# One issue order for every engine, taken from an offline list schedule, in an attention plus gated-FFT kernel; trigonometry folded onto PE and ACT; a 76-row score contraction

## Chip, cores and metric

The kernel runs on one core of a Trainium2 chip. The metric is device microseconds of one execution. A core has engines that run on their own and meet at semaphores: PE (matmul), DVE (vector), ACT (activations), POOL (GpSimd), and SP, whose queue here issues the transfers that are not weight loads. Times are medians of several executions; profiles are of one execution. A run counts as slow when it is over 1.5% above the fastest run of the same kernel.

## The reference

Block-sparse causal attention, then a gated long convolution done through an FFT over the sequence. Cut to what matters:

```python
B, H, S, D = 4, 8, 768, 64          # q, k, v: float32 [B, H, S, D]
k_rep = k.reshape(B, H, 12, 64, D).mean(axis=3)          # one mean key per block of 64
gate  = q @ k_rep^T, causal by block
keep  = the 3 best blocks of each query, plus its own block, and causal inside
attn  = softmax(where(keep, q @ k^T / 8, -1e9)) @ v
x     = attn as [B, S, 512]
x1, x2, x3 = split(x @ w_proj)                           # w_proj [512, 1536]
conv  = irfft(rfft(x2, axis=1) * rfft(filter, axis=0))   # over S
out   = (x1 * conv * x3) @ w_out                         # w_out [512, 512], float32
```

## The kernel before

Heads are handled in 16 pairs, four to a batch. Each pair passes through *prep* (PE transposes of q and k, block sums, gate matmuls, top-3 selection, a mask written as 12 extra rows beside the 64 rows of q and k), then *attention* (scores, exp, values, normalization, transposition into xT and its even and odd halves xe, xo). Each batch then passes through *hyena*: x2p projection, forward DFT with the multiplications of the spectrum, x13p projection, inverse DFT, output projection. While one batch's attention runs, the hyena of the batch before it runs between its pieces, and preps run two pairs ahead. The interleaving is a weighted merge of Python generators, and the build's scheduler re-sorts the merged program on all engines but SP:

```python
    def merge(streams):
        while True:
            live = [s_ for s_ in streams if s_.alive]
            if not live:
                return
            min(live, key=lambda s_: s_.key()).step()      # least advanced stream first
    ...
            streams = [Stream(attn_gen(st), T_ATT),
                       Stream(later_preps(b), NP * (T_PREP + 0.1))]
            ...
                streams.append(Stream(hyena_gen(prev), T_HY))
            merge(streams)
    ...
        with tc.manual_schedule(engines={mybir.EngineType.SP}):
            schedule()
```

Inside prep, the block sums become a float16 pair (kmb) on DVE, and the gate matmuls need them:

```python
            nc.vector.tensor_copy(km[r, 0, cc], ks[r, :])
            nc.vector.tensor_tensor(km[r, 1, cc], ks[r, :], km[r, 0, cc], op=ALU.subtract)
    ...
                nc.tensor.matmul(gn[:, 32 * c:32 * c + 24], lhsT=qx[:, P * c:P * (c + 1)],
                                 rhs=km[:, w, 0:24], start=(n_ == 0), stop=(n_ == 3))
```

Inside hyena, the spectrum comes first and the x13 projection only after it:

```python
        for c in range(HC):
            xa = ms_tile("xa")
            dft_fwd(x2[0], x2[1], c, 0, xa)
            nc.vector.tensor_mul(t1, xa, HA[:, c, :])      # and t4; then xb, t3, t2
            nc.gpsimd.tensor_add(Y[:, 3 * c + 1, :], t3, t4)
            re_eng.tensor_sub(Y[:, 3 * c, :], t1, t2)
        [... cut ...]
            for dc in range(DC):
                yield from x13(dc)
                yield from conv(dc)
```

Cosines and sines are made at the start: an outer product on PE, three DVE operations that reduce the angle, one ACT sine. The scores contract over all 128 rows of two tiles whose rows 64 to 127 were filled beforehand on DVE, ACT and POOL:

```python
                nc.vector.tensor_scalar(ka, in0=pr[:, 0:HS], scalar1=1.0 / S, scalar2=MAGIC,
                                        op0=ALU.mult, op1=ALU.add)
                nc.vector.tensor_scalar(kb, in0=ka, scalar1=-MAGIC, scalar2=-float(S),
                                        op0=ALU.add, op1=ALU.mult)
                nc.vector.tensor_tensor(kb, kb, pr[:, 0:HS], op=ALU.add)
                nc.scalar.activation(F[:, t, HS * hf:HS * (hf + 1)], kb, AF.Sin, bias=0.0,
                                     scale=TWO_PI / S)
```

The softmax here doesn't subtract the row's maximum and nothing guards it: scores larger than these inputs give would overflow.

Of the kernel before, what the change touches and what calls it, by code (L numbers as in the profile page):

```python
# [15 lines left out]

@with_exitstack
def kernel(
# [10 lines left out]
    nc = tc.nc  # L29

    B, H, S, D = q.shape
    P = 128
    NQ = S // P
    NB = S // 64
    NP = H // 2
    Dm = H * D
# [8 lines left out]
    MANUAL = False  # L45
    TWO_PI = 2.0 * math.pi

# [3 lines left out]
    qkT = ctx.enter_context(tc.tile_pool(name="qkT", bufs=2))  # L51
# [12 lines left out]
    tail = {"on": False, "n": 0}  # L64

# [3 lines left out]
    def ms_tile(name, dtype=FP32):  # L69
        if tail["on"]:  # L70
            tail["n"] += 1
            if tail["n"] % 3 == 0:
                return sc_tile(name)[:, 0:512]
        return ps_ms.tile([P, 512 if dtype == FP32 else 1024], dtype, name=name, tag="ms")


    id32 = const.tile([P, P], FP32)
    make_identity(nc, id32)
    id16 = const.tile([P, P], FP16)
    nc.vector.tensor_copy(id16, id32)  # L80

    NS = 6
# [3 lines left out]


    eblk = const.tile([P, S], FP16)
    nc.vector.memset(eblk[64:P, :], 0.0)
    nc.vector.memset(eblk[64:76, :], EMASK)  # L90
    nc.gpsimd.affine_select(
        out=eblk[64:76, :], in_=eblk[64:76, :], compare_op=ALU.is_ge,
        fill=0.0, base=0, pattern=[[1, S]], channel_multiplier=-64)
    nc.gpsimd.affine_select(
        out=eblk[64:76, :], in_=eblk[64:76, :], compare_op=ALU.is_ge,
        fill=0.0, base=63, pattern=[[-1, S]], channel_multiplier=64)

    for t_ in kmb:
        nc.vector.memset(t_, 0.0)

    def fill_slot_pool(sl):
        nc.gpsimd.memset(Qt[sl][64:P, :, :], 0.0)
        nc.gpsimd.affine_select(
            out=Kt[sl][64:P, :, :],
            in_=eblk[64:P, :].rearrange("p (o s) -> p o s", o=1).to_broadcast([P - 64, 2, S]),
            compare_op=ALU.is_ge, fill=0.0, base=0, pattern=[[0, 2], [0, S]], channel_multiplier=0)

    def fill_slot(sl):
        nc.vector.memset(Qt[sl][64:P, :, :], 0.0)
        for t in range(2):  # L110
            (nc.vector.tensor_copy if t else nc.scalar.copy)(Kt[sl][64:P, t, :], eblk[64:P, :])

    fill_slot(0)


# [7 lines left out]
    nc.vector.memset(rowv, 1.0)  # L123
    nc.vector.memset(colv, COS)
    nc.vector.memset(cv3[:, :, 1, :], SIN)
    nc.vector.memset(cv4[:, :, 1, :], SIN)
    nc.vector.memset(colv[:, P:P + 1], COS)
    nc.gpsimd.iota(rowv[0:1, :], pattern=[[1, HS]], base=0, channel_multiplier=0,  # L128
                   allow_small_or_imprecise_dtypes=True)
    nc.gpsimd.iota(cv3[0:1], pattern=[[1, 2], [0, 2], [2, P]], base=0, channel_multiplier=0,  # L130
                   allow_small_or_imprecise_dtypes=True)
    nc.gpsimd.iota(cv4[0:1], pattern=[[1, 2], [0, 2], [2, 64]], base=256, channel_multiplier=0,
                   allow_small_or_imprecise_dtypes=True)
    nc.vector.memset(colv[0:1, P:P + 1], 384.0)
    crow = const.tile([P, 1], FP32)
    nc.gpsimd.memset(crow, 2.0 / S)
    nc.gpsimd.memset(crow[0:1, :], 1.0 / S)
# [3 lines left out]

    def trig_gen():
        for t in range(HC):
            for hf in range(2):
                pr = ms_tile("trigp")
                nc.tensor.matmul(pr[:, 0:HS], lhsT=rowv[:, P * t:P * (t + 1)],
                                 rhs=colv[:, HS * hf:HS * (hf + 1)], start=True, stop=True)
                ka = hy2.tile([P, HS], FP32, name="trig", tag="ce")
                kb = hy2.tile([P, HS], FP32, name="kb", tag="prod", bufs=4)
                nc.vector.tensor_scalar(ka, in0=pr[:, 0:HS], scalar1=1.0 / S, scalar2=MAGIC,  # L150
                                        op0=ALU.mult, op1=ALU.add)
                nc.vector.tensor_scalar(kb, in0=ka, scalar1=-MAGIC, scalar2=-float(S),
                                        op0=ALU.add, op1=ALU.mult)
                nc.vector.tensor_tensor(kb, kb, pr[:, 0:HS], op=ALU.add)
                nc.scalar.activation(F[:, t, HS * hf:HS * (hf + 1)], kb, AF.Sin, bias=0.0,
                                     scale=TWO_PI / S)
                yield 1.2

    def trig_back():
        for t in range(6):  # L160
            gq = ms_tile("gq", FP16)
            for u in range(HC):
                nc.tensor.transpose(gq[:, P * u:P * (u + 1)], F[:, u, P * t:P * (t + 1)], id16)
            nc.vector.tensor_copy(G[:, t, :], gq[:, 0:HS])
            yield 0.2


# [4 lines left out]
    HA0 = const.tile([P, Dm], FP16)  # L172

    def dft_fwd(xe, xo, c, kind, pt):

        if c < 2:
            src = xe if c == 0 else xo
            col = 256 * c + 128 * kind
            for t in range(HC):
                nc.tensor.matmul(pt, lhsT=F[:, t, col:col + P], rhs=src[:, t, :],  # L180
                                 start=(t == 0), stop=(t == HC - 1))
        else:
            for t in range(HC):
                for r, src in ((0, xe), (64, xo)):
                    col = 512 + 2 * r + 64 * kind
                    nc.tensor.matmul(pt[r:r + 64, :], lhsT=F[:, t, col:col + 64],
                                     rhs=src[:, t, :], start=(t == 0), stop=(t == HC - 1),
                                     skip_group_check=True)

    fts = []  # L190

    def load_filter():
        for t in range(HC):
            f0 = hy2.tile([P, Dm], FP32, name="f0", tag="t", bufs=6)
            f1 = hy2.tile([P, Dm], FP32, name="f1", tag="t", bufs=6)
            nc.sync.dma_start(f0, moe_filter_fft[P * t:P * (t + 1), :])
            nc.sync.dma_start(f1, moe_filter_fft[HS + P * t:HS + P * (t + 1), :])
            fts.append((f0, f1))

    wsrc = moe_w_proj.rearrange("(c p) n -> p c n", p=P)  # L200

    def load_w(part):
        nc.gpsimd.dma_start(wp[:, :, Dm * part:Dm * (part + 1)], wsrc[:, :, Dm * part:Dm * (part + 1)])

    def filter_gen():
        yield from trig_back()
        fe = hy.tile([P, HC, Dm], FP16, name="x2e", tag="x2e")
        fo = hy.tile([P, HC, Dm], FP16, name="x2o", tag="x2o")
        for t, (f0, f1) in enumerate(fts):
            nc.gpsimd.tensor_tensor(fe[:, t, :], f0, f1, op=ALU.add)  # L210
            nc.vector.tensor_tensor(fo[:, t, :], f0, f1, op=ALU.subtract)
            yield 0.3
        for c in range(HC):
            sc = crow if c == 0 else 2.0 / S
            for kind, dst in ((0, HA), (1, HB)):
                pa = ms_tile("hf")
                dft_fwd(fe, fo, c, kind, pa)
                nc.scalar.activation(dst[:, c, :], pa, AF.Copy, bias=0.0, scale=sc)
                yield 0.64
        nc.vector.tensor_copy(HA0, HA[:, 0, :])  # L220
        nc.vector.tensor_copy(HA0[0:1, :], HB[0:1, 0, :])
        nc.vector.memset(HB[0:1, 0, :], 0.0)
        yield 0.1


    q_r = q.rearrange("b h (c p) d -> p (b h c) d", p=P)
    k_r = k.rearrange("b h (c p) d -> p (b h c) d", p=P)
    v_r = v.rearrange("b h (c p) d -> p (b h c) d", p=P)
    loaded, vas = {}, {}
    NG = B * NP  # L230

    def load_qk(g):
        qn = nat.tile([P, NQ, 2, D], FP32, name="qn", tag="qn")
        kn = nat.tile([P, NQ, 2, D], FP32, name="kn", tag="kn")
        for src, dst in ((k_r, kn), (q_r, qn)):
            for t in range(2):
                n = NQ * (2 * g + t)
                nc.sync.dma_start(dst[:, :, t, :], src[:, n:n + NQ, :])
        loaded[g] = (qn, kn)

    def load_v(g):
        n = slice(2 * NQ * g, 2 * NQ * (g + 1))
        vn = nat.tile([P, 2 * NQ, D], FP32, name="vn", tag="vn")
        nc.sync.dma_start(vn, v_r[:, n, :])
        vas[g] = vn

    def cast_v(g):
        va = gp.tile([P, 2, NQ, 65], FP16, name="va", tag="va", bufs=5)
        nc.gpsimd.memset(va[:, :, :, 64:65], 1.0)
# [3 lines left out]
        vas[g] = va  # L253
        return ins.ins

    def prep_gen(g):
        Qs, Ks, km = Qt[g % NS], Kt[g % NS], kmb[g % 3]
        qn, kn = loaded.pop(g)
        q2h = gp.tile([P, S], FP16, name="q2h", tag="q2h")
# [390 lines left out]
```

## Time and profile before

| | before |
|---|---|
| median | 307.97 us before the prediction, 306.24 us with the result's runs added |
| profiled span | 305.3 us |
| busy share | PE 83%, DVE 72%, ACT 58%, POOL 45% |
| start: to the first x2p matmul | 79.1 us |
| middle: first x2p matmul to the first one of the last batch | 184.0 us |
| end: the last hyena | 42.2 us |

From the page of the kernel before: the engine totals, three rows of the strip of 40 slices (a digit is a busy share in tenths; each slice here is 7.6 us), and the chain that ended last, by engine.

```profile
PE 254.0 (83%) x2309; PEld 153.9 (50%) x2309; DVE 218.7 (72%) x673; ACT 176.3 (58%) x277; POOL 138.0 (45%) x202
...
PE   3485897797999698987997798988996999899891
...
PEclk9999999997999789999999799999999899999999
DMA  9998999699387308276759119094902000310005
...
PE 43%; DVE 31%; POOL 8%; ACT 6%; DMA 5%; issue 4%; SPq 1%; ACTq 0%; DVEq 0%
```

No engine is full, yet the chain passes from one to another: the sign of a run bound by waits between engines. The PEclk row is not to be trusted before its first record, which in this trace comes at 37.8 us. Until then the distances of the matmuls tell the clock: float32 transposes stand 213 ns apart, and 109 ns later.

The same run by stages (window view; columns are stretch, length, busy us and instruction count of PE, PEld (PE's weight loads), DVE, ACT and POOL, granted clock, DMA share, GB/s). The DMA share is the summed time of all packets over that of 16 engines.

```profile
0.00:79.10 79.10, 56.13 (x551) 37.05 (x552) 60.15 (x219) 52.10 (x75) 44.91 (x78) 0.98 0.97 184
79.10:263.10 184.00, 164.98 (x1584) 100.91 (x1581) 134.41 (x416) 109.32 (x175) 87.71 (x121) 0.96 0.47 100
263.10:305.30 42.20, 32.92 (x179) 15.94 (x177) 24.10 (x40) 14.89 (x28) 5.40 (x4) 0.98 0.19 74
```

PE's busy time in these rows is modelled. I therefore counted PE work as the distances at which matmuls follow each other when nothing stops them (512 columns 215 ns, 384 columns 162, 128 columns 55, float32 transposes 109, value matmuls 31, gate matmuls 25). What a matmul takes beyond that is either half clock or a stall. By this count, an estimate, the middle holds 147.7 us of work, 6.7 us of half clock and 29.7 us of stalls.

One such stall, which returns in every batch. This is the chain of waits of the kernel before from 163 to 171 us (start, us, what):

```profile
163.14 0.60 DVE t_2720 L481
163.74 0.47 DVE ks L268
...
164.23 1.03 DVE kmb_112 L275
...
165.50 1.14 DVE kmb_112 L276
...
166.85 0.56 DVE xT L422
...
167.44 0.56 DVE q2l L286
168.00 0.55 DVE xe L424
168.55 1.34 DVE xo L425
169.89 0.48 DVE prod L510
...
170.41 0.40 PE gn L297 x10
```

PE waits for DVE, and DVE works through a queue in which the gate's operands, the next pair's xe and xo and the products of the spectrum (t) and of x13 (prod) stand one behind the other. One kmb cast of 64x12 elements takes 1.03 us there, the next one 0.18 us. POOL's timeline of the same stretch shows why:

```profile
163.98 2.62 POOL L488 TENSOR_TENSOR Y<-t_2721,t_2691 64x512 f16<-64x512 f32 x2
167.07 2.60 POOL L489 TENSOR_TENSOR Y<-t_2690,t_2720 64x512 f16<-64x512 f32 x2
```

### The profile page before, as it was taken

To read this page: it belongs to the slowest core of one execution; us is meant where nothing else is said; L and a number is where in the kernel's file an instruction comes from. 1 tells how busy PE (TensorE), PEld (TensorE's weight loads), DVE (VectorE), ACT (ScalarE), POOL (GpSimd) and SP (SyncE) were. 2 spreads that over 40 slices of the span, in tenths; PEclk is the share of its full clock that TensorE was granted. 3 is DMA by queue.
4 is the path that set the end of the run, shared out by engine and by line. 5 is a ranking of instruction groups with operands and counts; after the bars stand their busy time and mean duration, and the time that the engine had idled before them with its cause. 6 is when DMAs were issued, how large, how long until landed. Compare 5 with 4: busy or idle time off the path is not lost.

```text
span 305.3 us, 6432 instructions
## 1 busy us (share of the span) xinstructions
PE 254.0 (83%) x2309; PEld 153.9 (50%) x2309; DVE 218.7 (72%) x673; ACT 176.3 (58%) x277; POOL 138.0 (45%) x202
## 2 busy tenths in 40 slices
PE   3485897797999698987997798988996999899891
PEld 2332674464555366654654466544544566444430
DVE  7699985856589768665589768665599676339790
ACT  2349987584847435665856356656865467541314
POOL 7886226542339723532159453531188344205100
PEclk9999999997999789999999799999999899999999
DMA  9998999699387308276759119094902000310005
GB/s 169 215 261 198 140 210 179 144 173 201 72 152 139 73 1 164 50 150 201 179 104 184 29 34 178 5 268 151 196 19 50 4 6 3 139 67 2 0 0 206
DMA packets 87311, 36.00 MB, mean 118 GB/s; under 512 B 76936, under 2 KB 83440, under 8 KB 87280
## 3 DMA queue, kind: packets, MB, share of 16 engines
q1 hardware_dynamic: 85168, 33.50, 50.7%
q0 software_dynamic: 2112, 2.10, 4.7%
q8 instruction: 18, 0.29, 0.4%
q14 instruction: 13, 0.11, 0.1%
HBM read 24.64 MB, written 6.29 MB: 101 GB/s over the span
## 4 chain that ended last, share of the span: by engine, by line
PE 43%; DVE 31%; POOL 8%; ACT 6%; DMA 5%; issue 4%; SPq 1%; ACTq 0%; DVEq 0%
PE x13p L502 9%; PE sp L381 7%; PE x2p L462 6%; PE cv L519 4%; PE op L543 3%; PE po L400 3%; POOL Y L483 2%; DVE xe L424 2%; ACT ex L385 2%; PE gn L297 2%; DVE ks L268 2%; DMA Qt_104<-q2h 2%; PE qp L284 2%; PE kp L267 2%; DVE sd L526 2%
## 5 line engine op out<-in xcount | busy, mean ns | idle before, releaser
L385 ACT ACTIVATE ex<-sp 128x1024 f16<-128x1024 f32 (+1 forms) x96 | 86.9, 921 | 46.6 <-PE sp L381 42.9
L387 POOL TENSOR_SCALAR_AFFINE_SELECT ex<-ex 128x256 f16<-128x256 f16 x96 | 39.1, 413 | 105.4 <-ACT ex L385 104.8
L502 PE MATMUL x13p<-xT,wp 128*128 128x384 f16 x256 | 51.7, 337 | 4.9 <-DVE prod L510 1.4
L400 PEld LDWEIGHTS <-ex 128*128 128x128 f16 x672 | 33.4, 99 | 14.0 <-issue 2.3
L400 PE MATMUL po<-va,ex 128*128 128x65 f16 x672 | 38.4, 197 | 1.0 <-POOL ex L387 0.9
L502 PEld LDWEIGHTS <-wp 128*128 128x128 f16 x256 | 24.4, 99 | 21.0 <-issue 8.6
L543 PE MATMUL op<-wo,yT 128*128 128x512 f16 x96 | 24.5, 380 | 3.9 <-POOL yT L528 3.2
L528 POOL TENSOR_TENSOR yT<-prod,sd 128x768 f16<-128x768 f32 x12 | 21.7, 1810 | 5.1 <-DVE sd L527 5.1
L267 PE MATMUL kp<-id_91,kn 128*128 128x128 f32 x96 | 18.2, 308 | 4.8 <-DMA kn<-in_k_dram 4.8
L546 ACT COPY osb<-op 128x512 f32<-128x512 f32 x24 | 13.6, 589 | 14.6 <-PE op L543 12.3
L286 DVE SCALAR_TENSOR_TENSOR q2l<-qp,q2h 128x384 f16<-128x384 f32 x32 | 17.5, 553 | 6.0 <-ACT q2h L285 5.5
L284 PE MATMUL qp<-id_91,qn 128*128 128x128 f32 x96 | 18.7, 313 | 3.2 <-DVE xT L422 2.9
L268 DVE TENSOR_REDUCE ks<-kp 128x6 f32<-128x384 f32 x32 | 17.6, 551 | 4.7 <-PE kp L267 4.4
L519 PE MATMUL cv<-G,Y 128*128 128x384 f16 x96 | 20.9, 350 | 0.0
L285 ACT ACTIVATE q2h<-qp 128x384 f16<-128x384 f32 x32 | 15.7, 497 | 8.9 <-PE qp L284 8.2
L412 DVE TENSOR_TENSOR xn<-po,rec 128x384 f16<-128x384 f32 x32 | 17.8, 555 | 0.7
L250 POOL TENSOR_SCALAR_AFFINE_SELECT va<-vn 128x768 f16<-128x768 f32 x16 | 14.5, 903 | 5.5 <-DMA vn<-in_v_dram 5.4
L297 PEld LDWEIGHTS <-q2h 128*128 128x128 f16 x160 | 10.5, 101 | 12.3 <-issue 5.9
L284 PEld LDWEIGHTS qp<-id_91,qn 128*128 128x128 f32 x96 | 12.5, 160 | 7.7 <-DVE xT L422 4.1
L381 PE MATMUL sp<-Qt_104,Kt_98 128*128 128x512 f16 (+3 forms) x48 | 13.5, 373 | 2.8 <-DMA Qt_104<-q2h 1.4
L267 PEld LDWEIGHTS kp<-id_91,kn 128*128 128x128 f32 x96 | 11.8, 156 | 7.3 <-POOL rowv L128 4.7
L543 PEld LDWEIGHTS <-yT 128*128 128x128 f16 x96 | 8.1, 97 | 12.7 <-POOL yT L528 4.3
(318 smaller groups left out, 540.1 us busy)
## 6 DMA issues: line engine op xcount, KB each, us to landing
kn<-in_k_dram SPq DMA_DIRECT2D x32, 192.0 KB
qn<-in_q_dram SPq DMA_DIRECT2D x32, 192.0 KB
vn<-in_v_dram SPq DMA_DIRECT2D x16, 384.0 KB
out_dram<-osb SPq DMA_DIRECT2D x24, 256.0 KB
wp<-in_moe_w_proj_dram POOLq DMA_DIRECT2D x3, 512.0 KB, 6.4
Qt_104<-q2h SPq DMA_DIRECT2D x6, 96.0 KB
Qt_105<-q2h SPq DMA_DIRECT2D x6, 96.0 KB
Qt_106<-q2h SPq DMA_DIRECT2D x6, 96.0 KB
```

Source lines behind the costliest of these rows:

```text
L267: nc.tensor.transpose(kp[:, P * c:P * (c + 1)], kn[:, HC * hf + c, :, :], id32)
L268: nc.vector.reduce_sum(ks[:, 6 * hf:6 * hf + 6], kp[:, 0:HS].rearrange("p (n t) -> p n t", t=64), axis=AX.X)
L284: nc.tensor.transpose(qp[:, P * c:P * (c + 1)], qn[:, HC * hf + c, :, :], id32)
L381: nc.tensor.matmul(sp[:, col:col + w], lhsT=kt[:, P * kc:P * (kc + 1)], rhs=qt[:, q0:q0 + w], start=True, stop=True, skip_group_check=True)
L385: nc.scalar.activation(ex[:, 0:w], sp[:, 0:w], AF.Exp, scale=ESC)
L387: nc.gpsimd.affine_select(out=dv, in_=dv, compare_op=ALU.is_ge, fill=0.0, base=0, pattern=[[0, 2], [1, P]], channel_multiplier=-1)
L400: nc.tensor.matmul(po[:, 65 * c:65 * c + 65], lhsT=exs[pi][:, col:col + P], rhs=va[:, h % 2, kc, :], start=(kc == 0), stop=(kc == c), skip ...
L462: nc.tensor.matmul(pp, lhsT=src[:, dc, P * t:P * (t + 1)], rhs=wp[:, dc, Dm:2 * Dm], start=(dc == 0), stop=(dc == DC - 1))
L502: nc.tensor.matmul(xp[:, 0:HS], lhsT=wp[:, d2, base + P * dc:base + P * (dc + 1)], rhs=xT[:, d2, hs:hs + HS], start=(d2 == 0), stop=(d2 == ...
L519: nc.tensor.matmul(cv[:, 0:HS], lhsT=Y[:, 3 * par + n_, ds_], rhs=G[:, g_, :], start=(n_ == 0), stop=(n_ == 2))
L528: (nc.vector if last else nc.gpsimd).tensor_mul(yT[:, dc, :], prod, sd)
L543: nc.tensor.matmul(op, lhsT=yT[:, d2, P * c:P * (c + 1)], rhs=wo[:, d2, :], start=(d2 == 0), stop=(d2 == DC - 1))
```

## The change

The intent: write every piece of work as an operation in a named *strand* (prep of even and odd pairs, scores, values, x13, hyena, convolution and output, loads, and so on), let an offline list schedule find one order of all operations, store it as a string, and issue exactly that on every engine. Some operations are changed or moved at the same time. Core of the diff:

```diff
+QUEUES = ("Cg", "Fa", "Fg", "Fp", ..., "Xa", "Xp", "Xv")      # strand + engine
+ORDER = (';OTONNP;OP;ON;NON;CP;O;AC;NE;CE;CEAT5;...')          # 1357 operations
+    def op(strand, eng):
+        def put(fn):
+            queues.setdefault(strand + eng, deque()).append(fn)
+            ...
-        with tc.manual_schedule(engines={mybir.EngineType.SP}):
-            schedule()
+    with tc.manual_schedule():
+        for c_ in ORDER:
+            queues[QUEUES[ord(c_) - 48]].popleft()()
 [... cut: the same work, now as operations ...]
-            nc.vector.tensor_copy(km[r, 0, cc], ks[r, :])
+            e = POOL if KM_ENG(g) == "g" else DVE       # POOL for all pairs but the first
+            e.tensor_copy(km[r, 0, 12 * t:12 * t + 12], st["ks"][r, :])
-        eng = nc.gpsimd if st["b"] == 0 and j < NP - 1 else nc.vector
+        return "g" if j < NP - 1 else "v"               # xe, xo: POOL in every batch
-        (three DVE operations and a sine for each of six angle tiles)
+        ACT.activation(kas[t], pv(t), AF.Identity, bias=magic, scale=1.0 / S)
+        DVE.tensor_scalar(kbs[t], in0=kas[t], scalar1=-MAGIC, scalar2=None, op0=ALU.add)
+        PE.matmul(pv(t)[:, hf, :], lhsT=nsid, rhs=kbs[t][:, hf, :], start=False, stop=True)
+        ACT.activation(F[:, t, :], pv(t), AF.Sin, bias=0.0, scale=TWO_PI / S)
-        kt, qt = (x[(NP * st["b"] + h // 2) % NS][:, h % 2, :] for x in (Kt, Qt))
+        kt, qt = (x[(n // 2) % NS][0:KR, n % 2, :] for x in (Kt, Qt))       # KR = 76
-    fills of rows 64 to 127 on DVE, ACT, POOL
+    SP.dma_start(Kt[sl][64:KR, :, :], eblk[64:KR, :] ...)   # 12 rows, by transfer
+    the second pair, like parts of the first, is copied directly by ACT, not relayed by transfer
```

In the new order x13 operations stand inside the spectrum stage, and the previous batch's output projection is held back into the next spectrum, the last one too.

## The prediction

> **What bounds the kernel now.** No engine is full: the engine table gives PE 83%, DVE 72%, ACT 58%, POOL 45% of 305.3 us, and PE's busy time is modelled. From the start-to-start distances of warm back-to-back matmuls in the timeline (512 columns 215 ns, 384 columns 162, 128 columns 55, float32 transposes 109, value matmuls 31, gate matmuls 25) all PE work is about 216 us. The rest is start-up, drain and stalls. By stages:
>
> - 0 to 79 us (first x2p matmul): only 37 us of PE work. The 40-slice strip shows DMA at 85 to 100% (256-byte packets of q, k, v), and float32 transposes stand 213 ns apart until about 37 us, 109 ns afterwards. That agrees with the Trainium skill, "TensorE: Matmul & The Clock Gate", Part 1: the array runs at half clock until it has been kept busy.
> - 79 to 263 us: 148 us of PE work, 80% dense, 66 us per batch. The chain of waits leaves PE at the spectrum stage for DVE multiplications, POOL's Y sums, kmb casts, xT and xo; the clock halves four times for 3.4 to 6.8 us.
> - 263 to 305 us: the last hyena alone, 31 us of PE work in 42.
>
> **What the change does.** PE's work stays at about 217 us. The 76-row contraction saves PE nothing, since columns count; it removes fills of 64 rows (2.84 us each on POOL). DVE loses about 10 us of trigonometry, 19 us of kmb work and 12 us of xe/xo: some 45 of 219 us. POOL gains the last two, perhaps 35 us, and loses 11: near 165 us, not the bound. ACT stays near 175 us. The first pairs no longer go through a transfer (6.2 us in the chain at 11.7 us). The order is the large part: x13 matmuls go inside the spectrum stage, where PE stalls now, and the previous batch's output projection is kept as filler for the last spectrum.
>
> **Worth.**
> - Before the first x2p: 39 us of PE work, but the new order also prepares one pair more and loads all weights by then. The packets cost about 70 us at 16 busy engines (256-byte packets at 22 ns, weights at 112, relays at 108). I expect 72 us, 7 less.
> - First to last x2p: 144 us of PE work, at 89% density 162 us instead of 184.
> - Last hyena with filler: 33.6 us of work, 40 us with the drain, against 42.
>
> Sum 274 us.
>
> **Prediction: 274 us, 258 to 292 holding 8 times in 10. Faster by over 2%: 0.94; within 2%: 0.05; slower by over 2%: 0.01.**
>
> **What would show it right.** PE's modelled share about 90%; DVE busy about 175 us, POOL about 165; first x2p at 65 to 78 us; a batch (first x2p to the next) 56 to 60 us; half clock after 40 us nearly gone; DMA above 85% until the first x2p; more PE, less DVE in the chain.
>
> **What would make it wrong.** Faster: the start is not limited by DMA, or density reaches 95%. Slower: a fixed order lets each late transfer or slow POOL operation stop the engines behind it. The Trainium skill, "SBUF — State Buffer", "Who interferes with whom", says POOL and DVE share an exclusive port pair; the trace agrees loosely (kmb casts of one shape take 279 to 410 ns), so moving work to POOL may cost DVE what it saved.

## More of the kernel before

All PE waits that ended in the middle stage, by what ended them (total us, times, longest), the largest four:

```profile
PE gn L297 <- DVE prod L510: 4.6, 3, 1.5
PE op L543 <- POOL yT L528: 3.2, 3, 1.2
PE sp L381 <- ACT ex L385: 3.1, 5, 0.8
PE qp L284 <- DVE xT L422: 2.9, 3, 1.0
...
```

These are only the waits that the view lists; many short ones make up the rest of the 29.7 us.

Medians and profiles can hold a slow run, and the profile of the kernel before is a doubtful one: its run took 307.14 us, while the fast runs of that kernel in the result's call (304.50 and 301.81 us) average 303.2 us. Its granted clock, 0.97, is as high as that of runs of 301.5 us, so the clock does not explain it. Sums taken from that profile can thus be up to 4 us too long.

## The result, and the profile after

| | before | after |
|---|---|---|
| median | 306.24 us (301.81 to 308.21, 4 runs, 2 of them slow) | 275.00 us (273.92 to 276.44, 4 runs) |
| mean of the fast runs | 303.2 us (2 runs) | 275.1 us (4 runs) |
| ratio | | 0.907, 95% interval 0.897 to 0.918 |
| profiled span | 305.3 us | 273.7 us |
| start | 79.1 us | 81.2 us |
| middle | 184.0 us | 152.6 us |
| end | 42.2 us | 39.9 us |
| middle: PE work / half clock / stalls (estimate) | 147.7 / 6.7 / 29.7 us | 144.6 / 0.0 / 8.1 us |
| start: PE work / half clock / stalls (estimate) | 37.1 / 12.3 / 25.1 us | 39.2 / 17.0 / 20.3 us |

A ratio is the mean time of one kernel's fast runs over that of the other's fast runs of the same rounds, so it is not the ratio of the medians. Between fast runs the gain is 28.1 us. The half clock of the changed kernel's start, 17.0 us, is half of the 34.1 us of half-clock records in it, and so at most that. The rest of the start is the time before the first matmul.

The page of the changed kernel, the same rows as before (a slice is now 6.8 us):

```profile
PE 246.7 (90%) x2320; PEld 155.7 (57%) x2320; DVE 181.6 (66%) x581; ACT 176.3 (64%) x283; POOL 152.7 (56%) x273
...
PE   2859995598999999999999999999999999999984
...
PEclk9985696586899999999999999999999999999999
DMA  7999999967886092985912959761023300012106
...
PE 59%; POOL 11%; DVE 11%; ACT 7%; DMA 5%; issue 4%; SPq 0%; DVEq 0%; POOLq 0%; ACTq 0%
```

And its three stages in the window view, columns as above:

```profile
0.00:81.20 81.20, 61.50 (x586) 41.21 (x587) 46.55 (x191) 51.93 (x82) 37.79 (x91) 0.79 0.97 194
81.20:233.80 152.60, 150.63 (x1553) 97.59 (x1551) 108.05 (x351) 107.97 (x172) 106.99 (x178) 1.00 0.50 108
233.80:273.70 39.90, 34.60 (x185) 16.89 (x183) 27.04 (x41) 16.36 (x31) 7.87 (x6) 1.00 0.21 79
```

In these two profiles the gain lies in the middle: 31.4 us of 31.6 us. Up to 4 us of this may be the doubtful run of the kernel before, as e5's profile hints, so about 28 us is the gain to explain. The start did not get shorter at all, and the end gave 2.3 us. From the eleventh slice on, PE is at nine tenths or more until the last two slices, and the only PE wait that the view of waits lists for this stage of the changed kernel is (columns as above):

```profile
PE po L559 <- POOL ex L543: 1.8, 4, 0.6
```

How the order does it can be read from PE's timeline in the spectrum stage of the second hyena (start, busy us, line, operation, output, shapes):

```profile
138.76 0.81 PE L288 MATMUL xa<-x2e,F 128*128 128x512 f16 x3
139.41 0.83 PE L559 MATMUL po<-va,ex 128*128 128x65 f16 x21
140.07 0.65 PE L712 MATMUL cv<-G,Y 128*128 128x384 f16 x3
140.56 0.81 PE L633 MATMUL x13p<-xT,wp 128*128 128x384 f16 x4
141.21 1.03 PE L531 MATMUL sp<-Qt,Kt 76*128 76x512 f16 x6
142.17 0.45 PE L492 MATMUL mt<-id,nm 128*24 128x128 f16 x5
142.56 0.82 PE L288 MATMUL xb<-x2e,F 128*128 128x512 f16 x3
```

Between the two halves of one spectrum column stand work of the values, of the *previous* batch's inverse DFT, of x13, of the scores and of the mask. None of it needs what DVE is computing at that moment. The score matmuls now contract 76 rows, and with warm clock 512 columns follow each other at a median of 220 ns (216 before): fewer rows bought PE no time.

### The profile page after: what moved, and what is told of

Same layout as the page of the kernel before. It is cut to its first block, busy times and chain, and to the rows that moved or that the text cites. A ratio compares the mean times of both kernels' runs of the same rounds, so it can differ in the third digit from the quotient of the medians.

```text
span 273.7 us, 6448 instructions
## 1 busy us (share of the span) xinstructions
PE 246.7 (90%) x2320; PEld 155.7 (57%) x2320; DVE 181.6 (66%) x581; ACT 176.3 (64%) x283; POOL 152.7 (56%) x273
## 2 busy tenths in 40 slices
DMA packets 86839, 35.40 MB, mean 129 GB/s; under 512 B 76857, under 2 KB 82969, under 8 KB 86809
## 4 chain that ended last, share of the span: by engine, by line
PE 59%; POOL 11%; DVE 11%; ACT 7%; DMA 5%; issue 4%; SPq 0%; DVEq 0%; POOLq 0%; ACTq 0%
PE x13p L633 11%; PE sp L531 8%; PE x2p L616 7%; PE po L559 6%; PE op L749 6%; PE cv L712 4%; POOL Y L689 3%; PE qp L397 2%; ACT ex L537 2%; PE kp L354 2%; DMA vn<-in_v_dram 2%; POOL ex L543 2%; POOL x2e L305 2%; PE xa L288 2%; PE hf L288 2%
## 5 line engine op out<-in xcount | busy, mean ns | idle before, releaser
L537 ACT ACTIVATE ex<-sp 128x1024 f16<-128x1024 f32 (+1 forms) x96 | 85.5, 919 | 26.0 <-PE sp L531 24.3
L531 PE MATMUL sp<-Qt,Kt 76*128 76x512 f16 (+3 forms) x256 | 53.4, 321 | 1.2 <-ACT ex L537 1.2
L689 POOL TENSOR_TENSOR Y<-t,t 128x512 f16<-128x512 f32 (+1 forms) x28 | 35.6, 1279 | 14.7 <-DVE t L675 14.1
L531 PEld LDWEIGHTS <-Kt 76*128 76x128 f16 x256 | 23.4, 101 | 17.8 <-issue 5.1
L559 PE MATMUL po<-va,ex 128*128 128x65 f16 x672 | 29.7, 199 | 2.8 <-POOL ex L543 2.7
L559 PEld LDWEIGHTS <-ex 128*128 128x128 f16 x672 | 27.4, 101 | 7.2 <-POOL ex L543 3.7
L641 ACT CAST x<-x13p 128x384 f16<-128x384 f32 x32 | 15.3, 478 | 12.5 <-PE x13p L633 12.1
L647 DVE TENSOR_TENSOR prod<-x13p,x 128x384 f32<-128x384 f32 x32 | 17.7, 553 | 4.6 <-PE x13p L633 3.8
L397 PE MATMUL qp<-id,qn 128*128 128x128 f32 x96 | 17.0, 300 | 0.0
L372 ACT CAST k<-kp 128x384 f16<-128x384 f32 x28 | 13.3, 480 | 5.5 <-DVE ks L360 2.6
```

The lines of the kernel that those rows point to most:

```text
L397: PE.transpose(qp[:, P * c:P * (c + 1)], qns[g][:, HC * hf + c, :, :], id32)
L531: PE.matmul(sp[:, col:col + wd], lhsT=kt[:, P * kc:P * (kc + 1)], rhs=qt[:, q0:q0 + wd], start=True, stop=True, skip_group_check=True)
L537: ACT.activation(ex[:, 0:w], st[pi][:, 0:w], AF.Exp, scale=ESC)
L559: PE.matmul(po[:, 65 * c:65 * c + 65], lhsT=exs[n, pi][:, col:col + P], rhs=va[:, t, kc, :], start=(kc == 0), stop=(kc == c), skip_group_c ...
L689: (e.tensor_sub if neg else e.tensor_add)(st["Y"][o, row, :], st[x, c][r, :], st[y, c][r, :])
```

## The experiments

The runs came in four calls, each on one chip with its own runs of the kernel before, whose medians were 306.1, 306.1, 306.4 and 304.4 us. I compare variants of the changed kernel with its own 275.0 us across calls. The fast runs of the kernel before average 302.5, 303.6, 303.5 and 300.7 us in the four calls (303.2 us in the result's), so this is good to about 1 us, and to about 3 us for e12, the only run of the fourth call; the ratios are against the kernel before of the same rounds. "Start", "middle" and "end" are of the profiled execution.

| run | median us | ratio to before (95%) | start | middle | end |
|---|---|---|---|---|---|
| before (its profile is of the doubtful run) | 306.2 | 1 | 79.1 | 184.0 | 42.2 |
| changed kernel | 275.0 | 0.907 (0.897 to 0.918) | 81.2 | 152.6 | 39.9 |
| e1: changed, re-sorted by the scheduler | 287.7 | 0.951 (0.943 to 0.959) | 89.2 | 156.6 | 39.6 |
| e2: changed, kmb and xe/xo back on DVE | 282.1 | 0.933 (0.925 to 0.940) | 82.8 | 157.7 | 40.0 |
| e3: changed, large packets (wrong result) | 274.9 | 0.908 (0.901 to 0.915) | 81.7 | 152.2 | 40.0 |
| e4: changed, dummy matmuls | 270.4 | 0.895 (0.886 to 0.903) | 78.5 | 152.2 | 40.0 |
| e5: before, with the new operations | 303.4 | 0.999 (0.988 to 1.010) | 77.1 | 182.2 | 42.1 |
| e6: before, its order fixed | 333.7 | 1.099 (1.089 to 1.109) | 89.9 | 194.0 | 47.3 |
| e7: changed, x13 out of the spectrum | 281.8 | 0.929 (0.918 to 0.939) | 80.9 | 158.9 | 40.0 |
| e8: e4, and filter sums earlier | 268.1 | 0.883 (0.875 to 0.891) | 74.1 | 152.2 | 40.0 |
| e9: changed, filter sums earlier | 272.1 | 0.897 (0.890 to 0.904) | 78.7 | 152.2 | 40.0 |
| e10: e8, all weight loads later | 269.9 | 0.889 (0.879 to 0.898) | 71.9 | 157.0 | 40.0 |
| e11: e8 with large packets (wrong result) | 266.2 | 0.875 (0.864 to 0.886) | 75.6 | 152.2 | 39.9 |
| e12: e8, two weight loads later | 268.9 | 0.895 (0.889 to 0.902) | 72.2 | 153.9 | 40.0 |

All results but those of e3 and e11 were correct.

### Order or operations: e1, e5, e6

**e1.** The changed kernel, the scheduler deciding again.

```diff
-    with tc.manual_schedule():
+    with tc.manual_schedule(engines={mybir.EngineType.SP}):
```

> The changed kernel's operations, engines and buffers, but the compiler-side scheduler orders PE, ACT, DVE and POOL again, as in the kernel before; only the load queue keeps the fixed order. Theory A (the fixed order is what pays): the run loses most of the 31 us and lands at 292 to 308 us, first-to-last x2p again near 175 to 185 us. Rival B (the operations moved off DVE and the folded trigonometry pay, the order matters little): 272 to 282 us, with stage two near 153 us.

Measured: 287.7 us, below the range of theory A and above that of B. Neither won, and comparing the two built programs showed why: the scheduler started from the new order and kept 92% of PE's sequence of groups. (In the traces, PE's sequence of groups agrees with that of the changed kernel to 88% in e1 and to 29% in e5.) So e1 is no test of "the old order". What it does show is that letting the scheduler re-sort this order costs 12.7 us, 8.0 of them in the start.

**e5.** The other way round: the kernel before with its merge and its scheduler, and with the new operations.

```diff
+            e_ = nc.vector if g == 0 else nc.gpsimd
-            nc.vector.tensor_copy(km[r, 0, cc], ks[r, :])
+            e_.tensor_copy(km[r, 0, cc], ks[r, :])
-        eng = nc.gpsimd if st["b"] == 0 and j < NP - 1 else nc.vector
+        eng = nc.gpsimd if j < NP - 1 else nc.vector
-        kt, qt = (x[(NP * st["b"] + h // 2) % NS][:, h % 2, :] for x in (Kt, Qt))
+        kt, qt = (x[(NP * st["b"] + h // 2) % NS][0:KR, h % 2, :] for x in (Kt, Qt))
+ folded trigonometry, fills by transfer, direct copies for the second pair, as in the change
```

> The kernel before, with its own merge of streams and the scheduler deciding, but with all operations of the change: folded trigonometry, 76-row scores with fills by transfer, kmb and xe/xo on POOL, the second pair copied directly. It parts operations from order better than the scheduler run of the changed kernel, which was found to keep 92% of the new PE order. Theory A (order is the larger part): 290 to 300 us, first to last x2p 174 us or more. Rival B (operations are the larger part): 278 to 288 us, first to last x2p near 160 us.

Measured: 303.4 us, ratio 0.999. Theory A holds more strongly than it was put: in the old order, all the new operations together bought nothing that the interval can tell from zero. (Its profiled run, 303.1 us, is a typical one; that its stages look shorter than those of the kernel before is the doubtful profile of the latter.) DVE's busy time in the middle fell as it should, from 134 to 109 us, as the window view of e5 shows:

```profile
77.10:259.30 182.20, 163.42 (x1585) 101.47 (x1583) 108.74 (x358) 109.96 (x176) 111.12 (x180) 0.97 0.47 101
```

The relief turned into a new wait. PE's waits of e5's middle stage, to be held against those of before:

```profile
PE gn L308 <- POOL kmb L283: 7.9, 3, 2.7
PE op L559 <- POOL yT L544: 5.4, 3, 1.9
PE sp L397 <- ACT ex L401: 3.1, 5, 0.8
```

And POOL's timeline in e5 just before PE's gate matmul at 165.95 us:

```profile
159.77 2.60 POOL L504 TENSOR_TENSOR Y<-t,t 64x512 f16<-64x512 f32 x2
162.44 0.41 POOL L403 TENSOR_SCALAR_AFFINE_SELECT ex<-ex 128x256 f16<-128x256 f16 x1
162.81 2.59 POOL L505 TENSOR_TENSOR Y<-t,t 64x512 f16<-64x512 f32 x2
165.46 0.44 POOL L283 CAST kmb<-ks 64x12 f16<-64x12 f32 x2
```

The gate matmul waited for DVE before, last for a product of the x13 stage (prod); now it waits 2.7 us for kmb, which stands behind the spectrum's sums on POOL. The skill's page "Perfetto Trace Analysis", "Tensor Engine Instruction (MATMUL, LD_WEIGHTS)", calls ACT, DVE and GPSIMD strictly first-in first-out; the 0.44 us cast that had to wait behind 5.6 us of other POOL work agrees.

**e6.** The order of before, fixed.

```diff
-    MANUAL = False
+    MANUAL = True
 [... cut: two weight loads lose the hint that orders them after a cast of v ...]
```

> The kernel before with its merged order fixed on every engine, nothing else changed (two weight loads lose their ordering hint). If the scheduler's re-sorting is what costs (it cost 12.7 us on the changed kernel), this gains: 292 to 301 us. Rival: fixing an order is worth nothing unless the order itself is better, since each stall then holds the engine: 304 to 330 us.

Measured: 333.7 us, a little above the rival's range. A fixed order is not worth anything by itself: this one, fixed as it was merged, is 9.9% slower, and the scheduler had been repairing it. Together e1, e5 and e6 show that the gain needs the new order, and that this order is better issued as it stands. They do not show which features of the order matter.

### What in the order: e7

```diff
- ORDER: x13 operations of batches 0 to 2 inside their spectrum (15, 13 and 13 of 32)
+ ORDER: the same operations directly after that spectrum's last Y sum
```

> The changed kernel, only the x13 operations of batches 0 to 2 that stand before the end of that batch's spectrum are moved to directly after it (15, 13 and 13 of 32 each). Theory A1 (x13 inside the spectrum fills PE's waits): the stretch from first to last x2p grows by 3 to 5 us a batch, total 283 to 290 us. Rival A2 (score, value and projection work fills them as well): 274 to 278 us.

Measured: 281.8 us. The middle grew by 6.3 us, 2.1 us a batch; A1 expected 3 to 5 us a batch, A2 nothing. The x13 filler is thus worth about 7 of the 28 us. That the other fillers do most of the rest is likely, but no run takes them out. The PE waits of e7's middle stage show where part of it went:

```profile
PE po L559 <- POOL ex L543: 5.4, 6, 1.2
```

This is the wait of the changed kernel, 1.8 us there, three times as long; it accounts for 3.6 of the 6.3 us.

### What the moves between engines are worth in the new order: e2

```diff
-                e = POOL if KM_ENG(g) == "g" else DVE
+                e = DVE
-                e = POOL if XE_ENG(b, j) == "g" else DVE
+                e = POOL if b == 0 and j < NP - 1 else DVE
```

> The changed kernel in its fixed order, but the kmb work of all pairs and xe/xo of batches 1 to 3 are done on DVE again instead of POOL, at the same places in the order. DVE busy time should go from 182 back to about 210 us, POOL from 153 to about 125. Theory A (order pays): 274 to 280 us. Rival B (relief of DVE pays): 286 us or more, the loss lying in the stretch from first to last x2p.

Measured: 282.1 us, between the two theories: DVE was busy 206 us, POOL 126 us, as expected, and 5.1 us were lost in the middle. So moves that bought nothing in the old order (e5, together with the other new operations) are worth about 7 us in the new one. Why they do no harm there can be read from the trace of the changed kernel. The kmb operations still stand directly behind Y sums on POOL three times in the middle (at 96.05, 147.96 and 203.68 us), but PE's order has the gate matmuls 1.1 to 5.0 us after the kmb operations end, so PE never waits for them in this stage; in e5 PE stood waiting until kmb ended. Order and engine choice are not two separate gains that add.

### Why the start did not get shorter: e3, e4, e8 to e12

My prediction held the start to be bound by DMA packets. **e3** tests this with the same bytes in fewer packets (23,350 instead of 86,839 in the whole run), with rows permuted and the result therefore wrong.

```diff
-    q_r = q.rearrange("b h (c p) d -> p (b h c) d", p=P)
+    q_r = q.rearrange("b (g t) s d -> (b g) (t s d)", t=2).rearrange("g (p x) -> p g x", p=P)
 [... cut: k and v likewise; each transfer takes a contiguous run per partition ...]
```

> WRONG RESULT ON PURPOSE: q, k and v are read with the same bytes but as contiguous runs per partition (1,536 and 3,072 bytes instead of 256), so rows are permuted; everything else is the changed kernel. Theory D (my prediction's: the start is bound by DMA packets): first x2p moves from 81 us to 70 us or earlier and the total falls to 258 to 266 us. Rival L (the start is bound by latencies between engines and by the half clock of PE): DMA share before the first x2p falls clearly below 0.8, but first x2p stays at 78 to 83 us and the total within 272 to 277 us.

Measured: 274.9 us, and the first x2p at 81.7 us. The window view of e3's start:

```profile
0.00:81.70 81.70, 61.62 (x587) 41.57 (x588) 46.72 (x191) 52.05 (x82) 38.01 (x91) 0.83 0.73 193
```

The DMA share fell from 0.97 to 0.73 and the start did not move; between 50 and 60 us the share was 0.04 in e3, against 0.80 in the changed kernel. Nor does PE's view of waits name a transfer before the first x2p in either run. So the packets were not what the start waited for, and theory D fell. The bytes were not reduced (193 and 194 GB/s), so e3 is no test of these.

**e4** tests the half clock, by dummy matmuls in front of PE operations that had been seen to wait. (The expectation says 63; the kernel had 68.)

```diff
+    def keep_warm(n):
+        @op("Z", "p")
+        def _():
+            t = ms_tile("wm")
+            for _i in range(n):
+                PE.matmul(t, lhsT=wu[:, 0:P], rhs=wu, start=True, stop=True)
+    for n_ in (8, 3, 1, 3, 2, 4, 4, 3, 2, 1, 1, 1, 5, 2, 4, 12, 3, 2, 3, 1, 2, 1): keep_warm(n_)
```

> The changed kernel with 22 groups of dummy matmuls (63 in all, 512 columns, results never read), put in front of those PE operations of the start that were seen to wait. Theory L (half clock costs 17 us of the start and is set by PE's idle windows): half-clock stretches between 15 and 70 us shrink from 34 us to under 10 us, first x2p at 66 to 74 us, total 260 to 268 us. Rival D (DMA bounds the start): clock may rise, but first x2p stays at 79 to 84 us and total at 273 to 278 us.

Measured: 270.4 us, a gain of 4.6 us. The half-clock records between 15 and 70 us went from 34.1 to 6.8 us, but the first x2p only from 81.2 to 78.5 us (the profiled run, 272.5 us, is the slowest of e4's four). So theory L is half right: the clock is a cost, but most of the time that it freed did not shorten the run. How much of it went into the dummies themselves (68 of 215 ns, an estimated 14.6 us of PE time) was not separated.

The trace of the changed kernel names one wait of the start. POOL's timeline of it, in the changed kernel (start, busy us, line, operation, tiles, shapes, count, idle time before and its releaser):

```profile
47.65 0.91 POOL L596 TENSOR_TENSOR xe<-xT 128x384 f16<-128x384 f16 x1 [2.61 <-DVE xT L588]
48.51 3.38 POOL L305 TENSOR_TENSOR x2e<-f,f 128x512 f16<-128x512 f32 x2
```

and PE's timeline of the changed kernel at the same place:

```profile
50.27 0.58 PE L288 MATMUL hf<-x2e,F 128*128 128x512 f16 x1 [2.13 <-POOL x2e L305]
51.94 1.44 PE L288 MATMUL hf<-x2e,F 128*128 128x512 f16 x3 [1.08 <-POOL x2e L305]
```

POOL stood idle for 2.61 us for a transpose (xT), while two filter sums stood behind that xe in the fixed order; and PE, its next operation being a filter matmul, stood with it. **e8** and **e9** move the filter's remaining sums and differences (Fg, Fv) up, ahead of the values, the preps and xe (Vg), with and without the dummies; e8 has 59 dummies, since the wait at the filter is meant to go.

```diff
- ORDER: Cg Rv Vp Rv Rv Vv Rs Rv Vp Rp Ls Vv Rv Vg Fv Rs Fg Fv Fg Vg Fp
+ ORDER: Cg Fv Fg Fv Fg Rv Vp Rv Rv Vv Rs Rv Vp Rp Ls Vv Rv Vg Rs Vg Fp
```

> The kernel with dummy matmuls (270.4 us), and the filter's remaining half sums and differences on POOL and DVE are put before the value and xe/xo work that they stood behind in the fixed order. Theory F (the start is a chain of in-order waits, of which the filter stage is one: POOL stood idle for a transpose with filter work queued behind it): first x2p at 73 to 76 us, total 265 to 268 us. Rival: another chain bounds the start, first x2p stays at 77 to 80 us and total at 269 to 272 us.

> The changed kernel with only the filter's halves moved earlier in the fixed order, without dummy matmuls. From 270.4 to 268.1 us this move gained 2.3 us on top of the dummies. If the two gains add (filter stall and half clock are separate costs): 271.5 to 273.5 us. If they share a cause (the filter stall is what lets the clock fall at 42 us): 268 to 271 us. If the gain needs the warm clock: 274 to 276 us.

Measured: e8 268.1 us with the first x2p at 74.1 us; e9 272.1 us with 78.7 us. They lie where theory F and "the gains add" put them, e8 0.1 us past the end of its range: moving four operations in a list of 1,357 is worth 2.3 us with the dummies (of which e8 has nine fewer) and 2.9 us without. This is the price of a fixed order when one release comes later than it assumed.

In e8 the chain of waits of the start runs through transfers for much longer than before: filter and q and the issue of the filter make up 26% of its first 76 us. Its longest such pieces:

```profile
29.80 4.79 SPq L209
...
37.44 6.49 DMA f<-in_moe_filter_fft_dram
...
51.41 3.54 DMA qn<-in_q_dram
...
58.10 3.86 DMA qn<-in_q_dram
```

**e10** therefore issues the weights later, **e12** only two of them, **e11** repeats the large packets of e3 on e8.

```diff
- ORDER: the four weight loads at operations 2, 35, 93 and 108
+ ORDER e10: at about 216, 250, 285, 430      ORDER e12: at 2, 35, about 216, about 500
```

> The 268.1 us kernel with the four weight loads issued later (after about 40 us, the output weights after the first x2p), since its chain of waits now goes through the issue and landing of the filter and of q at 29 to 44, 51 and 58 us. Theory D2 (once latencies are shortened, transfers bind the start, and the weights stand before q and the filter): first x2p from 74 to 68 to 72 us, total 262 to 266 us. Rival: the same bytes are needed anyway, first x2p 73 to 76 us, total 267 to 270 us.

> WRONG RESULT ON PURPOSE: the 268.1 us kernel with q, k, v read in contiguous runs per partition (same bytes). On the changed kernel this bought nothing (274.9 us). Theory D2 (transfers bind the start once the waits between engines are shortened): first x2p at 72 us or earlier, total 263 to 266 us. Rival (DMA is still off the path): 267 to 269 us.

> The 268.1 us kernel with the first two weight loads at their original places and only the last two later (the third after the filter, the output weights after about 100 us). With all four late the first x2p came at 71.9 instead of 74.1 us, but a 5.4 us wait for v at 80 to 86 us, behind the crowded weights, gave the gain back. If that wait is the crowding's fault, both are avoided: first x2p 72 to 74 us, no PE stall above 1.5 us after it, total 265.5 to 267.8 us. If the order of the weights only moves the same wait about: 268 to 270 us.

Measured: e10 brought the first x2p to 71.9 us, as expected, but the middle took 157.0 instead of 152.2 us and the total was 269.9 us. Its trace shows why: POOL's cast of v waited 5.4 us for a late v, the exp masks stood behind it, and one value matmul waited 3.3 us for them, after which the clock fell to half for 6.8 us. In e12 the longest wait for v was 3.9 us and PE waited 1.0 us for the masks behind it (start 72.2 us, no wait of PE above 1.2 us after it), yet its six runs lie between 267.6 and 270.3 us and cannot be told from e8. e11, with fast runs of 264.3, 265.2 and 267.2 us and one slow one, its profile among them, is 2 to 3 us better than e8 on its own fast runs, but the intervals of the ratios overlap (0.864 to 0.886 against 0.875 to 0.891). Theory D2's first x2p of 72 us or earlier was not seen, but the only profile (75.6 us) is of the slow run. I take it that transfers now matter a little, not more; that is not shown.

The best correct version that was run is e8, 268.1 us, ratio 0.883 to the kernel before. It is 6.9 us below the changed kernel.

**Open.** What bounds the start after e8 is not settled: no single removal moved it by more than 5 us. The folded trigonometry, the 76 rows and the direct copies were tried only together (e5). Whether another merge order, without a list schedule, would reach the same middle was not tried.

## Why the prediction was right or wrong

The time was right: 274 predicted, 275.0 measured. That it was so close is luck: two terms of the sum were wrong by the same amount with opposite signs, the start by 9.2 us too short and the middle by 9.4 us too long.

- **"The order is the large part": right, shown.** All new operations in the old order gave 0.999 (e5). The old order fixed gave 1.099 (e6). In the new order the moves between engines are worth about 7 us (e2), and x13 in the spectrum about 7 us (e7).
- **"I expect 72 us" before the first x2p, since "the packets cost about 70 us at 16 busy engines": wrong, and this is the step that failed.** The first x2p came at 81.2 us, outside my 65 to 78. I took a busy share for a bound. e3 took away three quarters of the packets (share 0.97 to 0.73) and the start stayed at 81.7 us. The prediction had named "the start is not limited by DMA" as a way to be faster; it was not limited by packets, and was slower. What stood there instead: half clock, at most an estimated 17.0 us and 4.7 us more than before; and chains of short waits, of which the filter sums were one (e4, e8, e9).
- **"144 us of PE work, at 89% density 162 us": mechanism right, size wrong.** The work was 144.6 us and the middle 152.6 us, so the density was 95%. Waits of 8.1 us were left where I had allowed 18.
- **"40 us with the drain" for the end: right**, 39.9 us.
- **What would show it right.** PE's share 90%: right. DVE 175 and POOL 165 us: 181.6 and 152.7 us, the direction right and the sizes off. The 60 kmb operations took 209 ns on POOL, not the 290 or more that they averaged on DVE, which makes 5 of POOL's 12 us; the rest was not traced. A batch in 56 to 60 us: the three intervals from x2p to x2p are 48.0, 57.2 and 47.4 us, and the kernel before had 65.9, 66.0 and 52.1 us, so one figure for all batches was no good measure. Half clock after 40 us nearly gone: wrong in the start (20.5 us of it between 42.6 and 69.9 us), right after it (none). (Of the four halvings that the prediction put between 79 and 263 us of the kernel before, one, at 71.9 us, lies in the start.) DMA above 85% until the first x2p: right as the mean of the window view (0.97), not in the last four slices before it (6, 7, 8 and 8 tenths); and it proved nothing, as e3 shows, the less as this share can pass 1. More PE and less DVE in the chain: right, 59% against 43% and 11% against 31%.
- **"Moving work to POOL may cost DVE what it saved."** In the new order it did not (e2). In the old order the moves bought nothing (e5), and there PE waited for the queue on POOL. The page "SBUF — State Buffer", "Who interferes with whom", calls the ports that DVE and POOL share an exclusive lock, and the kernel before agrees far more closely than the prediction put it (its 279 to 410 ns are means). Of the 64 kmb operations on DVE, 51 took 152 to 170 ns; the other 13 took 329 to 1125 ns, and each of them ended within 0.03 us of the end of an instruction on POOL. xe and xo on DVE took 0.36 and 0.35 us undisturbed, and up to 1.60 and 1.42 us beside work on POOL. By the excess over the undisturbed times, an estimate, these three lost 17 us of DVE's 219 us in the kernel before. The move takes these operations out of that conflict; how much of the 7 us of e2 this makes was not tested by itself.

## What to carry to other kernels

When no engine is full and the chain of waits passes from one to another, relieving one engine may only move the wait; look first at what stands behind what in each queue, and at whether a slow operation is slow by itself or held by another engine, and put independent work between a producer and its consumer. A fixed order pays only if it is a better order, and then a single late release in it costs every engine behind it, so read the trace once more and move the few operations that others wait behind. Before you call a stage bound by DMA, or by any busy queue, take the load away in a run, even with a wrong result, and see whether the stage moves.

## What the Trainium skill lacked or had wrong

- "TensorE: Matmul & The Clock Gate", Part 1, says that the clock falls after at least one idle window of about 3.4 us. In the changed kernel it fell after windows in which PE was far from idle: by the distances of its matmuls, PE streamed for 37%, 42% and 43% of the three windows that ended at 18.7, 42.6 and 63.1 us, and the longest single stall in them was 1.2 us. The same part tells of a kernel whose short idle times between groups made the clock swing, but gives no share below which a window counts as idle.
- The same page, the same part, puts the ramp penalty below 1% of a typical kernel's span. That is the ramp at the start of a kernel; here the clock fell three more times in the start. Half clock there is an estimated 17.0 of 273.7 us at most, and dummy matmuls that took away 27 of the 34 us of half-clock records after 15 us gained 4.6 us (1.7%).
- "GPSIMD Engine Reference", 4.1 Engine selection, advises VectorE for elementwise work, with GPSIMD about twice as slow for two-input operations. At 128x512 float32 the trace agrees (1.26 us on POOL against 0.67 us on DVE). For the 64x12 operations on kmb the difference is far smaller: medians of 190 ns (cast) and 208 ns (subtraction) on POOL in the changed kernel, against 171 and 169 ns on DVE in e2, whose mean of 292 ns comes from the operations that POOL's work held, up to 1.12 us. The page has nothing on such small tiles.
- No page that I read ties the worth of a move between engines to the order of issue: under the unchanged order of e5 the wait for DVE's queue became one for POOL's (ratio 0.999). Nor does one say that fixing an order that a scheduler had been repairing can cost 9.9% (e6).
